# A tuned adaLN block on one core: one tile's exponentials, the second gate's column and its spread moved to other places

## The chip, the core and the metric

The kernel is one program on one core of a Trainium2 chip. Its matrix work is done by TensorE (PE, with PEld for the loading of weights); VectorE (DVE), ScalarE (ACT) and GpSimd (POOL) do the rest, and SyncE (SP) issues most of the DMA transfers. Each engine takes its own instructions in its own order; semaphores tie them together.

The metric is the device time in microseconds of one execution. The kernel before took 769.94 us (median of 3 runs, 769.52 to 769.98).

## The reference

One transformer block on x of 2048 tokens by D = 640, modulated by a condition c. All is in f32.

```python
mod = silu(c) @ w_mod                      # six rows of 640: sa, ca, ga, sb, cb, gb
h = layernorm(x) * (1 + ca) + sa
q, k, v = h @ wqkv                         # 32 heads of 20
phi(z) = concat(softmax(z @ w_phi), softmax(-(z @ w_phi)))    # per head, 40 features
o = (phi(q) @ (phi(k).T @ v)) / (phi(q) @ sum(phi(k)) + 1e-6) # linear attention
x = x + ga * (o @ wo)
h = layernorm(x) * (1 + cb) + sb
out = x + gb * (relu(h @ w1 + b1) ** 2 @ w2 + b2)             # F = 1728
```

Two rows of `mod` matter here: gb, the second gate, by which the MLP's result is multiplied, and b2, the MLP's last bias, which enters as gb * b2.

## The kernel before

Products are made to f32 accuracy from operands that are split into a rounded high part and the remaining low part (`lo` at L87), as three matmuls each. Tokens go in 16 tiles of 128, two tiles to a pair, so there are 8 pairs.

Four stages follow one another. First, up to about 230 us, weights are prepared and every tile gets its k, v and q; phi(k) is accumulated against v, and of phi(q) the exponentials of tiles 0 to 11 are written to DRAM. The last four tiles (`KEPT` = 12 and up, so 12 to 15) keep their q in `EQ`, and their softmax work is done later: `q_chain(t, False)` (DVE: maximum and minimum per head, then two differences, L430 to L433), `exps` (ACT, two exponentials, L436 and L437) and `q_sums` (DVE, sum per head, L478).

Second, a short stretch turns the accumulated products into `kvd`, `kv5` and `zb`. Here the column form of the second gate is begun: `mod_turn(5, ...)` leaves it as `mt5`, one row buffer of the tag s1, of which there are five, and `biases()` reads b2 into another (`b2s`, L510).

Third, the loop over pairs at L1134, in which `b` and `c` are the tiles 2j+5 and 2j+6 that DVE works on ahead of PE. For each tile, `e_prod` (DVE product with zb and a reduction, L877 and L879, then small steps on POOL), `e_recip` and `e_scale` (L892 to L906) make e', the scaled exponentials. For each pair, `tr_e` transposes e' on PE in six groups (`te`, L921), ACT evicts each (`ept`, L923 or L925); `num` multiplies them with kvd and kv5 into the numerator (`numa`, `numb`, `numc`); `num_hi` (ACT, L950) and `num_lo` (DVE, L957) split it into `ot`; and `do_wo` multiplies it with the gated output weights (`pwo`, evicted as `at`, L982). Three PSUM banks are shared by the groups and the numerator. The order of PE, DVE, ACT and POOL in this loop is the order of the program text; SP's order is left to the planner, which goes by its own estimates of when a transfer is ready. `SPREAD` says after which pair a kept tile's `q_chain` and `exps` come, `SUMS` in which pair its `q_sums`. At the end of pair 3, `mod_sum(5, gate_b)` (DVE, L310) sums the turned gate into a column of 5 chunks, and `spread_row` writes this column to DRAM (L328) and reads it back as a row on all partitions, `gb_b` (L329). In pair 5 DVE makes `bb` = b2 * gb_b (L1149). The raw rows of w1 and w2 are loaded by `p_load` (SP, L1004 and L1007), copied by `p_hi` (ACT, L1014) and `p_lo` (DVE). The last pair contains the first layer norm's transposes for the MLP (`t2(0, ...)`, `tb`).

Fourth, from about 389 us to the end, the MLP over pairs j and steps n of two chunks of F each: `up` (PE), its relu and square (ACT L1250, DVE L1251), rounding and low part (`ra`), then the products with w2 one step behind (`acc`, `acc3x`). The order of all five engines is written out by hand for the first pair. `bb` is first used by `add_bias` at step 6 of the first pair, gb_b when the first pair ends.

Of the kernel before, what the change touches and what calls it, by code (L numbers as in the profile page):

```python
# [51 lines left out]
def kernel(  # L52
# [64 lines left out]
    def row(tag, name):  # L117
        return (pc if tag in ("s3", "s4") else mem).tile([P, D], F32, tag=tag, name=name, bufs=BUFS[tag])
# [316 lines left out]
    def exps(e):  # L435
        nc.scalar.activation(e[:, 0], e[:, 0], AF.Exp)  # L436
        nc.scalar.activation(e[:, 1], e[:, 1], AF.Exp, scale=-1.0)  # L437
# [65 lines left out]
            nc.gpsimd.dma_start(w[2 * n : m, 0], w[2 * n : m, 1])  # L503

    ga_b = row("s4", "ga_b")
    b2s = []

    def biases():
        b2s.append(row("s1", "b2s"))
        nc.sync.dma_start(b2s[0], bass.AP(tensor=b2.tensor, offset=b2.offset, ap=[[0, P], [1, D]]))  # L510

    GB = []

# [19 lines left out]
    }  # L533
    gate_a = const.tile([P, NC], F32, name="gate_a")
    gate_b = const.tile([P, NC], F32, name="gate_b")
    LAST_COL = {7: (2, gate_a), 9: (3, cols_b[:, 0:5]), 11: (4, cols_b[:, 5:10])}
    SIDE = {
        2: lambda: mod_mac(2, 0, 1, 2),
# [544 lines left out]
    def t2(j, *ds):  # L1083
        if 0 in ds:
            H2[j] = ht(f"h2_{j}", j, (0, 96))
        if j == 0:
            t_unit(XM[j], cols_b, H2[j], ds[0], f"b{j}", bank(f"tb{j}_{ds[0]}"))
            return
        p = tp(f"tb{j}_{ds[0]}")
        for k, d in enumerate(ds):  # L1090
            t_in(XM[j], d, p[:, 256 * k : 256 * k + 256])
        for k, d in enumerate(ds):
            t_out(cols_b, H2[j], d, f"b{j}", p[:, 256 * k : 256 * k + 256], XX[j][d % 2][:, :256])
# [35 lines left out]
    e_scale(3)  # L1129
    load_e(6)  # L1130
    e_prod(4)
    SPREAD, SUMS = {1: 1, 3: 2}, {2: 1, 4: 2}
    ln0 = None
    for j in range(NB):  # L1134
        nxt = j + 1 < NB
        b, c = 2 * j + 5, 2 * j + 6
        te_at = (0, 1) if 0 < j < 6 else (1, 2)
        if j == 4:
            load_x1(0)
        if j < 5:  # L1140
            p_load()
        if j != 5:
            e_prod(b)
        e_recip(b - 1)
        e_scale(b - 1)
        if j == 5:
            q_chain(KEPT + 3, False)
            add_x(0, 0, 1)
            nc.vector.tensor_tensor(bb, b2s[0], gb_b, op=ALU.mult)  # L1149
            ln0 = ln_parts(XM[0], "b0")  # L1150
        load_e(b + 2)
        def te(at):
            for i, gs in enumerate((range(3), (5, 3, 4))):
                if nxt and te_at[i] == at:
                    tr_e(j + 1, gs)

        do_wo(j, 0, 0)
        te(0)
        if j == 5:
            exps(EQ[KEPT + 3])  # L1160
            q_sums(KEPT + 3)
            e_prod(b)
        do_wo(j, 0, 1)
        if j == 7:
            t2(0, 0)
            t2(0, 1)
        te(1)
        if j == 5 or j == 6:
            next(ln0)
        if j in SUMS:  # L1170
            q_sums(KEPT + SUMS[j])
        e_prod(c)
        if j != 5:
            e_recip(b)
            e_scale(b)
        do_wo(j, 1, 0)
        if j == 7:
            t2(0, 2)
            t2(0, 3)
        te(2)  # L1180
        if nxt:
            num(j + 1)
            num_hi(j + 1)
        do_wo(j, 1, 1, 0, 8)
        if j == 7:
            t2(0, 4)
        if not nxt:
            do_wo(j, 1, 1, 8, 16)
        if nxt:
            do_wo(j, 1, 1, 8, 11)  # L1190
            num_lo(j + 1)
            do_wo(j, 1, 1, 11, 16)
        if j == 5:
            e_recip(b)
            e_scale(b)
        if j in SPREAD:
            q_chain(KEPT + SPREAD[j], False)
            exps(EQ[KEPT + SPREAD[j]])
        if j == 3:
            mod_sum(5, gate_b)  # L1200
            spread_row(1, gate_b, gb_b)
        load_e(c + 2)
        if j == 5:
            next(ln0)
        if 1 <= j < 6:
            p_hi()
        if j == 5:
            p_lo(4)
            p_load(4)
        if j == 6:  # L1210
            p_hi(4)
            p_lo(5)
            p_load(3)
        if j == 7:
            p_load(2)
# [315 lines left out]
    for j in range(NB):  # L1531
        if j <= PLAIN:
            if j:
                by_hand.__exit__(None, None, None)
            by_hand = tc.manual_schedule(engines={ET_.PE, ET_.DVE, ET_.Activation, ET_.Pool} | ({ET_.SP} if j != 1 else set()))
            by_hand.__enter__()
        for n in range(NP):
            down = lambda k: prev and (down_plain if plain(*prev) else down_pair)(*prev, k)
            twice = not plain(j, n)
            m = NP * j + n - NP - 1  # L1540
            if (j, n) == (NB - 1, NP - 1):
                for k in range(2):
                    up(j, 2 * n + k)
                    split_a(j, n, (k,))
                for i in range(2):
                    add(Y[j][i], Y[j][i], XR[j, i])
                break
            done = j - 1 if j and prev else None
            up(j, 2 * n)
            if prev and not plain(*prev):  # L1550
                split_s(*prev)
            down(0)
            if j < PLAIN:
                layer(j + 1, 2 * n, None if j else 0)
            if 0 < m < NP - 2:
                t_split(m - 1)
            if m == -1:
                t_load(0)
            if (j, n) == (PLAIN, 0):
                t_fetch(4)  # L1560
            if j >= PLAIN:
                if n == 5 + (j == PLAIN):
                    for i in range(2):
                        add_bias(j, i)
                layer(j + 1, 2 * n)
            prep(next(PREPS, 0))
            if j == 0:
                layer(j + 1, 2 * n, 1)
            if n == 0 and j:
                if j - 1 >= PLAIN:  # L1570
                    first_combos(j - 1)
                else:
                    Y[j - 1] = [row("s2", f"y{j - 1}_{i}") for i in range(2)]
                for r, i, c in (("3", 0, R), ("2", 0, L)):
                    end(j - 1, r, i, c)
            if n == 1 and j:
                gate(j - 1, 0)
                if j != PLAIN:
                    finish(j - 1, j < PLAIN)
            if n == 1 and j == PLAIN:  # L1580
                finish(j - 1, 0)
            if n == 2 and j == PLAIN:
                t_sums(NP - 2)
            if n == (2 if j > PLAIN else 1) and j:
                gate(j - 1, 1)
            if n == (5, 5, 5, 3)[min(j, 3)]:
                residual(j)
            for i in range(2):
                if n == 6 and j == 0:
                    add_bias(j, i)  # L1590
            if j == NB - 1 and n == 1:
                for k in range(NP - LAST, NP - 1):
                    plain_load(k)
            if j == NB - 1 and n == 3:
                for k in range(NP - LAST, NP - 1):
                    plain_split(k)
            if j == NB - 1 and n == NP - 2:
                for i in range(2):
                    by_gate(Y[j][i], Y[j][i], slice(0, D))
            up(j, 2 * n + 1)  # L1600
            if j >= PLAIN and n == 0:
                down(1)
            split_a(j, n)
            if twice:
                sums(j, n)
            if j < PLAIN or n:
                down(1)
            if m == NP + 1:
                t_split(NP - 2)
            ahead = (j, n) == (0, 3)  # L1610
            if ahead:
                layer(j + 1, 2 * n + 1)
            prep(next(PREPS, 0))
            if n == 0 and j:
                end(j - 1, "4", 1, L)
                end(j - 1, "x", 1, R)
            if n == (2 if j > PLAIN else 1 if j == PLAIN else 0) and j:
                finish(j - 1, j >= PLAIN)
            if not ahead:
                layer(j + 1, 2 * n + 1)  # L1620
            if 0 <= m < NP - 2:
                t_sums(m)
            if m == NP - 2:
                t_split(m - 1)
            if 0 < m + 1 < NP - 1:
                t_load(m + 1)
            if m == NP - 1:
                for i in range(2):
                    add_bias(j - 1, i)
            if j == NB - 1 and n == NP - LAST:  # L1630
                first_combos(j)
            prev = j, n
# [60 lines left out]
```

## Time and profile before

| what | value |
|---|---|
| median of 3 runs | 769.94 us |
| the profiled execution | 769.86 us, span 768.2 us |
| PE busy | 759.3 us (99%) |
| PEld busy | 739.8 us (96%) |
| DVE busy | 593.8 us (77%) |
| ACT busy | 434.6 us (57%) |
| POOL busy | 144.2 us (19%) |
| TensorE clock granted | 1.000 |

Rows of the order of time read: start and duration in us, engine, line of the kernel, operation, tile written and tiles read, shapes, count. A bracket gives the idle time before it and what ended that. Matmuls are pipelined, so a busy PE in such rows overlaps its neighbour, and the distance between two starts is the better measure of what a piece of work takes.

### The profile page before, as it was taken

To read this page: it belongs to the slowest core of one execution; us is meant where nothing else is said; L and a number is where in the kernel's file an instruction comes from. 1 tells how busy PE (TensorE), PEld (TensorE's weight loads), DVE (VectorE), ACT (ScalarE), POOL (GpSimd) and SP (SyncE) were. 2 spreads that over 40 slices of the span, in tenths; PEclk is the share of its full clock that TensorE was granted. 3 is DMA by queue.
4 is the path that set the end of the run, shared out by engine and by line. 5 is a ranking of instruction groups with operands and counts; after the bars stand their busy time and mean duration, and the time that the engine had idled before them with its cause. 6 is when DMAs were issued, how large, how long until landed. Compare 5 with 4: busy or idle time off the path is not lost.

```text
span 768.2 us, 15300 instructions
## 1 busy us (share of the span) xinstructions
PE 759.3 (99%) x5967; PEld 739.8 (96%) x5967; DVE 593.8 (77%) x1083; ACT 434.6 (57%) x971; POOL 144.2 (19%) x301
## 2 busy tenths in 40 slices
PE   9999999999999999999999999999999999999997
PEld 8999999999999989888999999999999999999996
DVE  6598897989999999999565667866767666675666
ACT  5766756767843454545776647465553636445331
POOL 3001101101100255442101000231321313222110
PEclk9999999999999999999999999999999999999999
DMA  9811431343333344155356367996766758766450
GB/s 327 305 65 73 137 103 54 104 139 114 119 104 109 117 142 170 70 80 160 107 180 222 110 226 253 286 323 195 226 181 197 232 177 262 221 184 192 130 165 35
DMA packets 52151, 126.69 MB, mean 165 GB/s; under 512 B 7335, under 2 KB 8103, under 8 KB 52079
## 3 DMA queue, kind: packets, MB, share of 16 engines
q1 hardware_dynamic: 34744, 84.65, 33.1%
q0 software_dynamic: 14752, 35.76, 16.7%
q10 hardware_dynamic: 2583, 5.30, 1.8%
q8 instruction: 47, 0.77, 0.4%
q14 instruction: 25, 0.20, 0.1%
HBM read 95.70 MB, written 29.89 MB: 163 GB/s over the span
## 4 chain that ended last, share of the span: by engine, by line
PE 85%; DVE 8%; issue 2%; DMA 2%; POOL 2%; ACT 1%; SPq 0%; POOLq 0%; DVEq 0%
PE up L78 23%; PE acc L78 17%; PE pk L78 9%; PE pv L78 9%; PE pq L78 8%; PE pwo L78 5%; PE acc3x L78 5%; PE kvp L450 3%; DVE dn L879 2%; DVE scr L877 2%; DVE ezb L901 1%; PE tb L357 1%; PE te L921 1%; DMA ring_b<-td_b 1%; PE ta L357 1%
## 5 line engine op out<-in xcount | busy, mean ns | idle before, releaser
L78 PE MATMUL up<-h,w 128*128 128x256 f32 x1640 | 206.4, 278 | 0.0
L78 PEld LDWEIGHTS up<-h,w 128*128 128x128 f32 x1640 | 196.1, 188 | 0.0
L1250 ACT ACTIVATE ft<-up,b_t 128x256 f32<-128x256 f32 x104 | 48.9, 470 | 115.1 <-PE up L78 114.6
L78 PE MATMUL acc<-w,ra 128*128 128x384 f32 x452 | 97.4, 335 | 0.0
L1251 DVE TENSOR_TENSOR ft<-ft 128x256 f32<-128x256 f32 x104 | 44.1, 424 | 51.2 <-ACT ft L1250 49.6
L78 PE MATMUL pwo<-wo,ot 128*128 128x256 f32 (+3 forms) x512 | 80.8, 312 | 0.6 <-DVE ot L88 0.6
L78 PEld LDWEIGHTS pwo<-wo,ot 128*128 128x128 f32 (+1 forms) x512 | 74.5, 188 | 3.8 <-issue 2.7
L78 PE MATMUL pq<-wq,hT 128*128 128x384 f32 (+1 forms) x480 | 75.2, 312 | 0.0
L78 PEld LDWEIGHTS acc<-w,ra 128*128 128x128 f32 x452 | 72.7, 188 | 0.7 <-DVE ra L88 0.5
L78 PE MATMUL pk<-wk,hT 128*128 128x384 f32 (+1 forms) x480 | 72.7, 308 | 0.0
L78 PE MATMUL pv<-wv,hT 128*128 128x384 f32 (+1 forms) x480 | 71.7, 307 | 0.0
L78 PEld LDWEIGHTS pq<-wq,hT 128*128 128x128 f32 x480 | 71.1, 188 | 0.6 <-issue 0.2
L78 PEld LDWEIGHTS pk<-wk,hT 128*128 128x128 f32 x480 | 70.5, 188 | 0.4 <-issue 0.2
L78 PEld LDWEIGHTS pv<-wv,hT 128*128 128x128 f32 x480 | 70.1, 188 | 0.0
L88 DVE TENSOR_TENSOR ra<-ft,ra 128x384 fp32r<-128x384 f32 (+2 forms) x86 | 36.8, 448 | 32.9 <-ACT ra L1274 20.2
L78 PE MATMUL acc3x<-w,ra 128*128 128x256 f32 x248 | 42.3, 278 | 1.4 <-DVE end L1418 1.4
L1360 POOL DMA_DIRECT2D ring_a<-td_a x34 | 18.3, 537 | 125.5 <-PE acc L78 103.2
L1274 ACT ACTIVATE ra<-ft 128x384 fp32r<-128x384 f32 x48 | 25.2, 526 | 28.4 <-DVE ft L1251 22.4
L78 PEld LDWEIGHTS acc3x<-w,ra 128*128 128x128 f32 x248 | 39.5, 188 | 1.8 <-DVE end L1418 1.6
L1265 DVE TENSOR_TENSOR ft<-ft 128x128 f32<-128x128 f32 x136 | 33.3, 286 | 1.2
L441 DVE TENSOR_REDUCE sk<-ek 128x64 f32<-128x1280 f32 x16 | 23.7, 1484 | 12.4 <-ACT ek L436 10.8
L885 POOL TENSOR_TENSOR dn<-dn,rs_q 128x32 f32<-128x32 f32 x32 | 20.1, 629 | 68.1 <-DVE dn L879 67.8
(264 smaller groups left out, 1406.5 us busy)
## 6 DMA issues: line engine op xcount, KB each, us to landing
ring_c<-td_c POOLq DMA_DIRECT2D x34, 384.0 KB, 4.0
ring_a<-td_a POOLq DMA_DIRECT2D x34, 384.0 KB, 4.1
ring_b<-td_b POOLq DMA_DIRECT2D x34, 256.0 KB, 4.0
esp<-eq SPq DMA_DIRECT2D x12, 640.0 KB, 3.2
el<-esp SPq DMA_DIRECT2D x12, 640.0 KB, 4.0
rw<-in_w SPq DMA_DIRECT2D x23, 320.0 KB, 3.1
wm<-in_w_mod SPq DMA_DIRECT2D x20, 320.0 KB, 3.7
xb<-in_x SPq DMA_DIRECT2D x8, 640.0 KB, 4.0
```

The lines of the kernel that those rows point to most:

```text
L78: nc.tensor.matmul(o, a, b, start=first and i == 0, stop=last and i == len(terms) - 1, skip_group_check=skip,)
L88: (eng or nc.vector).tensor_tensor(out_lo, full, hi.bitcast(F32), op=ALU.subtract)
L357: nc.tensor.transpose(p[:, i * P : (i + 1) * P], xn[:, i, d * P : (d + 1) * P], ident)
L441: nc.vector.tensor_reduce(s, heads(flat(e)), axis=AX.X, op=ALU.add)
L450: nc.tensor.matmul(kvp[g // 4][64 * c : 64 * c + 64, a : a + 2 * n].rearrange("p (s n) -> p s n", s=2), v[:, u], e[:, :, o : o + n], start ...
L877: nc.vector.tensor_tensor(z, flat(ET[t]), flat(zb), op=ALU.mult)
L885: nc.gpsimd.tensor_tensor(dn[:, s], dn[:, s], rs[:, 1 - s], op=ALU.mult)
L1250: nc.scalar.activation(r, p, AF.Relu, bias=b1_t[:, f : f + 1])
L1251: nc.vector.tensor_tensor(r, r, r, op=ALU.mult)
L1265: nc.vector.tensor_tensor(t[:, o], t[:, a], t[:, b], op=op)
L1274: nc.scalar.activation(a[:, 0, :3], t[:, :3], AF.Copy)
L1360: nc.gpsimd.dma_start(RING[j, n, r], TD[n][r].bitcast(F32R))
```

## The change

- `exps` of kept tile 13 move from the end of pair 1 into pair 2, after its second group of e' transposes; the sums of tile 13 (`q_sums`) move from pair 2 to pair 3. Tile 14 keeps its places.
- `mod_sum(5, gate_b)` moves from the end of pair 3 to the start of pair 6.
- Instead of writing the column to DRAM as it stands, TensorE turns it in pair 7 (`gbt`, into the PSUM tile of the tag tp), ACT copies it to a new small tile `gate_r` of 5 rows by 128, and SP writes those rows and reads `gb_b` back.
- b2 is read into `bb` itself, which frees the row buffer of `b2s`; the product bb * gb_b moves from pair 5 to the MLP's first pair, step 4.
- Where the first group of e' transposes comes at place 0 (pairs 1 to 5), the second takes its groups in the order 3, 4, 5 instead of 5, 3, 4.

```diff
     ga_b = row("s4", "ga_b")
-    b2s = []
-
+    
     def biases():
-        b2s.append(row("s1", "b2s"))
-        nc.sync.dma_start(b2s[0], bass.AP(tensor=b2.tensor, offset=b2.offset, ap=[[0, P], [1, D]]))
+        nc.sync.dma_start(bb, bass.AP(tensor=b2.tensor, offset=b2.offset, ap=[[0, P], [1, D]]))
...
     gate_b = const.tile([P, NC], F32, name="gate_b")
+    gate_r = pc.tile([NC, P], F32, name="gate_r")
...
-    SPREAD, SUMS = {1: 1, 3: 2}, {2: 1, 4: 2}
+    SPREAD, SUMS = {1: 1, 3: 2}, {3: 1, 4: 2}
...
         e_recip(b - 1)
         e_scale(b - 1)
+        if j == 6:
+            mod_sum(5, gate_b)
         if j == 5:
             q_chain(KEPT + 3, False)
             add_x(0, 0, 1)
-            nc.vector.tensor_tensor(bb, b2s[0], gb_b, op=ALU.mult)
             ln0 = ln_parts(XM[0], "b0")
         load_e(b + 2)
         def te(at):
-            for i, gs in enumerate((range(3), (5, 3, 4))):
+            for i, gs in enumerate((range(3), (3, 4, 5) if te_at[0] == 0 else (5, 3, 4))):
...
         if j == 5 or j == 6:
             next(ln0)
+        if j == 2:
+            exps(EQ[KEPT + 1])
         if j in SUMS:
             q_sums(KEPT + SUMS[j])
...
         if j == 7:
             t2(0, 4)
+            p = tp("gbt")[:NC, :P]
+            nc.tensor.transpose(p, gate_b, ident)
+            nc.scalar.activation(gate_r, p, AF.Copy)
+            nc.sync.dma_start(GD[1], gate_r)
+            nc.sync.dma_start(gb_b, GD[1].rearrange("c p -> (c p)")[None, :].to_broadcast([P, D]))
...
         if j in SPREAD:
             q_chain(KEPT + SPREAD[j], False)
-            exps(EQ[KEPT + SPREAD[j]])
-        if j == 3:
-            mod_sum(5, gate_b)
-            spread_row(1, gate_b, gb_b)
+            if j > 1:
+                exps(EQ[KEPT + SPREAD[j]])
...
             if not ahead:
                 layer(j + 1, 2 * n + 1)
+            if (j, n) == (0, 4):
+                nc.vector.tensor_tensor(bb, bb, gb_b, op=ALU.mult)
```

## The prediction

> **What bounds the kernel now.** I read the page's first two parts, then busy time by windows over the attention output stage, then the order of time of each engine there, because only an order of time shows which wait ends last. In the page, the second list is the span in 40 slices of 19.2 us; in the windows each row gives PE, PEld, DVE, ACT and POOL busy time.
>
> ```profile
> PE   9999999999999999999999999999999999999997
> DVE  6598897989999999999565667866767666675666
> 300.00:320.00 20.00, 19.59 (x146) 16.79 (x143) 19.62 (x29) 10.45 (x24) 7.64 (x17) 1.00 0.29 100
> 320.00:340.00 20.00, 20.00 (x153) 18.45 (x152) 19.21 (x27) 10.38 (x22) 6.74 (x12) 1.00 0.44 86
> 340.00:360.00 20.00, 19.43 (x141) 17.18 (x142) 19.69 (x32) 9.71 (x21) 6.38 (x11) 1.00 0.58 141
> ```
>
> PE is in its nines everywhere, so the whole program is one long run of matmuls. From about 175 to 365 us DVE is full as well. There the two engines pass work to each other, and a microsecond is won only where PE stands still. So I looked for PE's standstills by comparing the same piece of work in successive pairs (pairs count from 0: pair 2 starts near 304, pair 3 near 319, pair 4 near 334; numerator n belongs to pair n and is made during pair n-1).
>
> ```profile
> 307.36 2.13 PE L78 MATMUL pwo<-wo,ot 128*128 128x256 f32 x16
> 309.82 1.63 PE L921 MATMUL te<-ident,ezb 128*80 128x128 f32 x10 [0.33 <-ACT ept L923]
> 311.20 3.02 PE L78 MATMUL pwo<-wo,ot 128*128 128x384 f32 x16
> ...
> 323.04 2.08 PE L78 MATMUL pwo<-wo,ot 128*128 128x256 f32 x16
> 325.98 3.08 PE L78 MATMUL pwo<-wo,ot 128*128 128x384 f32 x16
> ...
> 331.73 4.89 PE L78 MATMUL pwo<-wo,ot 128*128 128x256 f32 x32
> 336.46 1.48 PE L921 MATMUL te<-ident,ezb 128*120 128x128 f32 x12
> ...
> 346.52 2.46 PE L78 MATMUL pwo<-wo,ot 128*128 128x256 f32 x18
> 349.55 2.71 PE L78 MATMUL pwo<-wo,ot 128*128 128x384 f32 x14 [0.57 <-DVE ot L88]
> 352.11 0.49 PE L921 MATMUL te<-ident,ezb 128*120 128x128 f32 x3
> ```
>
> Output projection half plus second group of e' transposes takes 3.84 us in pair 2 (311.20 - 307.36) and 2.94 in pair 3 (325.98 - 323.04): pair 2 stands still for **0.90 us**, and the bracket names ACT's eviction of e'. Two projection halves up to the next transposes take 5.59 at the end of pair 4 (352.11 - 346.52) and 4.73 at the end of pair 3: **0.86 us** stand still there, for DVE's low part of the numerator. PE can win 1.76 us here, no more.
>
> Now why, from ACT and DVE.
>
> ```profile
> 306.91 0.74 ACT L436 ACTIVATE eq<-eq 128x640 f32<-128x640 f32 x1 [2.99 <-DVE eq L433]
> 308.19 0.72 ACT L1014 ACTIVATE w<-rw 128x640 fp32r<-128x640 f32 x1
> ...
> 315.71 0.60 ACT L950 ACTIVATE ot<-numa 128x512 fp32r<-128x512 f32 x1
> ...
> 311.96 1.47 DVE L478 TENSOR_REDUCE rs_q<-eq 128x64 f32<-128x1280 f32 x1
> ...
> 318.30 0.30 DVE L906 TENSOR_TENSOR ezb<-el,dn 128x80 f32<-128x80 f32 x1
> 318.52 0.68 DVE L88 TENSOR_TENSOR ot<-numa,ot 128x512 fp32r<-128x512 f32 x1
> 320.38 1.47 DVE L877 TENSOR_TENSOR scr<-el,zb 128x1280 f32<-128x1280 f32 x1
> ...
> 330.48 0.29 DVE L906 TENSOR_TENSOR ezb<-el,dn 128x80 f32<-128x80 f32 x1
> 331.19 0.69 DVE L88 TENSOR_TENSOR ot<-numa,ot 128x512 fp32r<-128x512 f32 x1 [0.42 <-ACT ot L950]
> 333.21 0.80 DVE L430 TENSOR_REDUCE mxq<-eq 128x32 f32<-128x640 f32 x1
> 336.37 0.81 DVE L310 TENSOR_REDUCE gate_b<-mt 128x5 f32<-128x640 f32 x1
> 337.10 1.48 DVE L877 TENSOR_TENSOR scr<-eq,zb 128x1280 f32<-128x1280 f32 x1
> ...
> 348.82 0.68 DVE L88 TENSOR_TENSOR ot<-numa,ot 128x512 fp32r<-128x512 f32 x1
> ```
>
> ACT sits 2.99 us in front of the kept tile's exponentials, and e' evictions stand behind them. PE, held up, brings the next numerator late, and DVE then waits 0.42 at 331.19.
>
> **The change, part by part.** The sum is made against the profiled run, 769.86 us (span 768.2), 0.08 under the median 769.94.
>
> *Exponentials of tile 13 from the end of pair 1 into pair 2.* They leave 306.91 and stand behind pair 2's second group of evictions. The copy at 308.19 no longer waits for DVE, evictions start when PE is ready, and the 0.90 us at 309.82 goes. What becomes late next: ACT's eviction of numerator 3, now behind them. The pair costs 1.28 (308.19 - 306.91), so that eviction starts at 315.71 - 0.90 + 1.28 = 316.09 and ends 0.60 later, at 316.69. DVE, without the sum of tile 13 ahead of it, comes at 318.52 - 1.47 = 317.05. Cover 0.36 us, so nothing; uncovered it costs up to the difference, see the rivals.
>
> *Sum of tile 13 from pair 2 to pair 3.* 1.47 us on DVE (311.96) leaves before 318.52 and comes back before 331.19: neutral for numerator 4. Its reader is e_prod(13) in pair 4, still later.
>
> *Effect on DVE at numerator 4.* From L906 to the first instruction after the low parts takes 2.08 in pair 2 (320.38 - 318.30) and 2.73 in pair 3 (333.21 - 330.48). The 0.65 difference is waiting for late PE; PE being 0.90 earlier, it goes: **-0.65 us**.
>
> *Second gate's column sum from pair 3 to pair 6.* DVE loses 337.10 - 336.37 = **-0.73 us** before numerator 5. So DVE reaches 348.82 by 1.38 earlier. PE, 0.90 earlier, still waits there; its wait of 0.86 falls to 0.86 + 0.90 - 1.38 = 0.38. The start at 349.55 moves by 1.38: **DVE, not PE, sets this gain.**
>
> ```profile
> 375.79 0.69 DVE L88 TENSOR_TENSOR ot<-numa,ot 128x512 fp32r<-128x512 f32 x1 [5.75 <-ACT ot L950]
> 423.60 0.42 DVE L1251 TENSOR_TENSOR ft<-ft 128x256 f32<-128x256 f32 x1 [0.34 <-ACT ft L1250]
> 387.83 0.38 PE L357 MATMUL tb<-ident,xm 128*128 128x128 f32 x2
> 387.97 1.19 PE L78 MATMUL pwo<-wo,ot 128*128 128x256 f32 x8
> 389.00 5.28 PE L78 MATMUL up<-h,w 128*128 128x256 f32 x45
> ```
>
> In pair 6 the sum lies in DVE's 5.75 us of idling: nothing; without it, 0.73. The row that it reads keeps its buffer until about 370 instead of 336.37, while b2, read straight into its final place, frees another of the five; one raw weight row then loads later, and its copy stands in the MLP's first pair, after 389.00. Nothing; should it be late after all, ACT waits as in rival C.
>
> *Product of b2 and the gate from pair 5 to the MLP's first pair, n=4.* In pair 5 PE no longer depends on it, so no gain. At its new place it fills the 0.34 idle before 423.60 and pushes that product by about 0.4; the pair's next step, the rounding of both halves, waits for a second product that comes a whole up step later. Nothing; 0.73 if that cover were gone.
>
> *The transposed column.* One TensorE transpose in pair 7, on PE's path. Two transposes hold back the next matmul by 387.97 - 387.83 = 0.14 and their neighbours' gaps bring it near 0.2; the bounds for one are 0.07 and 0.38 (the busy time of two). I take **+0.11**. ACT's small copy and DMA issues are off the path (below).
> The Trainium skill, page "TensorE: Matmul & The Clock Gate", section "Part 4: PE-mode transpose", gives some 275 ns for a transpose inside a kernel; charged in full the total would be 768.8. The row's starts say that neighbours overlap, so I keep the row.
>
> *Order 3, 4, 5 of the e' groups.* The same instructions; the short group goes last and its predecessors find banks free a little later. Between -0.1 and +0.1; taken as 0.
>
> *SP.* The gate's column and its spread leave pair 3 and come at the end of pair 7.
>
> ```profile
> 337.21 0.38 SPq L328 DMA_DIRECT2D gate<-gate_b  x1
> 348.77 0.33 SPq L329 DMA_DIRECT2D gb_b<-gate  x1
> 392.90 0.33 SPq L1004 DMA_DIRECT2D rw<-in_w  x1
> DMA to landing us min/median/max: 3.0/4.5/5.9
> 396.45 1.36 ACT L1014 ACTIVATE w<-rw 128x640 fp32r<-128x640 f32 x2
> 390.92 0.47 ACT L1250 ACTIVATE ft<-up,b_t 128x256 f32<-128x256 f32 x1 [0.78 <-PE up L78]
> ```
>
> The column write as 640 single words held SP's next step for 11.56 us (348.77 - 337.21), with no engine waiting. The new write is five rows. ACT's copy, some 0.4 us by its neighbours, eats into the 0.78 idle before 390.92; with that idle starting at 390.14 the write issues near 390.1 - 1.27 = 388.9. If the spread stands ahead of the raw row now issued at 392.90 (then 391.6), it holds that row once the write takes over 2.7 us. Bounds: 3.0 (the quickest raw row's landing) and 11.56. Five contiguous rows resemble a raw row: 3.0, so the row is 0.3 to 0.7 late. Its copy is the second of 396.45, at about 397.1: 4.2 us after issue, against landings from 3.0. Up to 1.2 of cover: nothing.
> By the Trainium skill, page "DMA: Bandwidth & Descriptors", sections "Specifications" and "Anatomy of one DMA", pieces under 512 B are read, modified and rewritten, and a transfer has a fixed cost of about 2.0 us; the new write has pieces of 512 B. By that SP would not be held at all; the total is the same.
>
> **Sum:** -1.38 + 0.11 = -1.27; 769.86 - 1.27 = 768.6 us, or 0.17% less. Later stages are PE-bound and shift as a whole. The measurement tells about 0.2%, 1.54 us, from no change, and this is under it. Own range 768.2 (the 1.76 us all won, less 0.11) to 769.1 (rival B).
>
> **The rivals.**
> *A: more is won than I count.* For it: PEld is busy 16.79 and 17.18 us in the windows with standstills, 18.45 in the one between; 1.66 + 1.27 = 2.93 us, less 0.11, gives 767.0. Against it: the windows hold different mixes of matmuls, and DVE allows 1.38. Between 767.0 and 768.2.
> The Trainium skill, page "Perfetto Trace Analysis", section "Identifying the Most-Contended Engine", prefers weight-load busy time over matmul busy time as the measure of headroom; that is the reading which gives this rival.
>
> *B: a new wait replaces the old.* If PE does not come the 0.90 earlier in pair 2, numerator 3 is evicted at 315.71 + 1.28 + 0.60 = 317.59, and DVE at 317.05 stands 0.54 us. The gain is 1.38 - 0.54 - 0.11 = 0.73: 769.1. If the 0.65 at numerator 4 also stays, 0.08: 769.8. Against it: ACT's 2.99 idle shows that it was DVE it waited for.
>
> *C: slower, through SP's queue.* If the five-row write takes as long as the column did and the spread stands ahead of the raw row, SP is held to 388.9 + 11.6 = 400.5, the row lands at median 4.5 later, 405, where its copy wanted it at 395.8. ACT stands 9.2 us with all activations of the MLP's next matmuls behind it. PE has at most a stretch like the 45 matmuls of 5.28 us in hand: 3.9 us lost, 772.5. It decides from a write of about 4 us on. For it: a gate write has been that slow. Against: that one was in single words.
>
> *D: placement.* Buffers of small tiles and raw rows move to other addresses and SP's order is the planner's. No row prices this: -0.5 to +2 around the forecast, 769.1 to 770.6 where it costs.
>
> **How the numbers follow.** Forecast 0.58; A 0.12; B 0.15; C 0.06; D 0.09. The likeliest is 768.6. Leaving out C, half of A and half of D gives 767.8 to 769.8. Faster than 768.4: A and a quarter of the forecast, 0.27. Slower than 771.5: C and a little of D, 0.08. The rest, 0.65, is within 0.2%.
>
> **What would show it.** Right: no ACT wait of some 3 us before the first L436 after 303; the second e' group of pair 2 following its projection in about 2.95 us; no DVE wait on numerators 3 and 4; L310 at about 369 inside DVE's idle time; the last pair's up matmuls starting near 387.7 instead of 389.00. Wrong: a DVE wait for ACT's numerator 3; PE's wait at numerator 5 still 0.86 or more; ACT's weight copies waiting for raw rows after 390; a gate write over 4 us.

## The result, and the profile after

| what | before | after |
|---|---|---|
| median of 14 runs each | 769.96 us (769.07 to 771.25) | 768.12 us (767.39 to 769.30) |
| ratio | | 0.998, 95% interval 0.9972 to 0.9987 |
| the profiled execution | 769.86 us, span 768.2 us | 768.32 us, span 766.6 us |

The interval is a gain of 1.0 to 2.2 us; 768.6 was forecast, from a gain of 1.27. In the timelines below, as in the prediction, a row gives start and duration in us, engine, line, operation, tiles, and in a bracket the idle time before it. First the order of time of TensorE in the changed kernel: the pieces of work that the prediction compared, and the one of pair 4.

```profile
307.05 2.08 PE L78 MATMUL pwo<-wo,ot 128*128 128x256 f32 x16
...
309.98 3.08 PE L78 MATMUL pwo<-wo,ot 128*128 128x384 f32 x16
...
336.34 2.08 PE L78 MATMUL pwo<-wo,ot 128*128 128x256 f32 x16
338.57 1.39 PE L920 MATMUL te<-ident,ezb 128*120 128x128 f32 x10 [0.15 <-ACT ept L922]
339.72 3.07 PE L78 MATMUL pwo<-wo,ot 128*128 128x384 f32 x16
...
345.46 5.29 PE L78 MATMUL pwo<-wo,ot 128*128 128x256 f32 x32
350.58 1.47 PE L920 MATMUL te<-ident,ezb 128*120 128x128 f32 x12
```

Pair 2's half and second group now take 2.93 us (309.98 - 307.05) where they took 3.84: the standstill there is gone. In pair 4 the same piece takes 3.38 (339.72 - 336.34), and the bracket names ACT's eviction of e'. At the end of pair 4, two halves up to the next transposes take 5.12 (350.58 - 345.46) instead of 5.59; 0.39 over the unhindered 4.73 is still lost. The kernel before, TensorE in pair 4:

```profile
337.69 2.13 PE L78 MATMUL pwo<-wo,ot 128*128 128x256 f32 x16
...
340.78 3.07 PE L78 MATMUL pwo<-wo,ot 128*128 128x384 f32 x16
```

So pair 4 took 3.09 before (340.78 - 337.69), and 0.29 us of standstill is new there. Now the order of time of ACT, then of DVE, in the changed kernel.

```profile
313.69 0.38 ACT L924 ACTIVATE ept<-te 80x256 f32<-80x256 f32 x1 [2.65 <-PE numa L78]
313.97 0.72 ACT L436 ACTIVATE eq<-eq 128x640 f32<-128x640 f32 x1
...
315.60 0.59 ACT L949 ACTIVATE ot<-numa 128x512 fp32r<-128x512 f32 x1
...
335.66 0.74 ACT L436 ACTIVATE eq<-eq 128x640 f32<-128x640 f32 x1 [2.75 <-DVE eq L433]
```

```profile
316.95 0.68 DVE L88 TENSOR_TENSOR ot<-numa,ot 128x512 fp32r<-128x512 f32 x1
...
330.52 0.68 DVE L88 TENSOR_TENSOR ot<-numa,ot 128x512 fp32r<-128x512 f32 x1
...
347.27 0.68 DVE L88 TENSOR_TENSOR ot<-numa,ot 128x512 fp32r<-128x512 f32 x1
...
368.12 0.82 DVE L310 TENSOR_REDUCE gate_b<-mt 128x5 f32<-128x640 f32 x1
374.21 0.69 DVE L88 TENSOR_TENSOR ot<-numa,ot 128x512 fp32r<-128x512 f32 x1 [5.28 <-ACT ot L949]
...
421.69 0.82 DVE L1627 TENSOR_TENSOR bb<-bb,gb_b 128x640 f32<-128x640 f32 x1
422.43 0.42 DVE L1256 TENSOR_TENSOR ft<-ft 128x256 f32<-128x256 f32 x1
423.93 0.43 DVE L88 TENSOR_TENSOR h<-xx,h 128x256 fp32r<-128x256 f32 x1 [1.09 <-ACT h L369]
```

Tile 13's exponentials follow the sixth e' group with no idle time (313.97), and numerator 3 is still evicted by 316.19 (315.60 + 0.59), 0.76 us ahead of DVE's 316.95. No bracket stands at numerators 3 and 4. DVE reaches numerator 5 at 347.27 instead of 348.82. The column sum lies in idle time, which shrank from 5.75 to 5.28, and the product of b2 pushes one product, ahead of 1.09 us of idling. The last fences: SP and TensorE around the gate's write.

```profile
388.46 0.28 SPq L1192 DMA_DIRECT2D gate<-gate_r  x1
389.65 0.33 SPq L1193 DMA_DIRECT2D gb_b<-gate  x1
391.42 0.33 SPq L1003 DMA_DIRECT2D rw<-in_w  x1
```

```profile
386.47 0.27 PE L1190 MATMUL gbt<-ident,gate_b 128*5 128x128 f32 x1
386.50 1.18 PE L78 MATMUL pwo<-wo,ot 128*128 128x256 f32 x8
387.51 5.28 PE L78 MATMUL up<-h,w 128*128 128x256 f32 x45
```

The five-row write let SP's next step go after 1.19 us (389.65 - 388.46), and the raw row stands at 391.42, 1.48 earlier than before's 392.90, as everything around it is.

**How the two traces are compared below.** The same matmul has a start in each trace. From the difference I take off the difference at matmul 100 (counted from 0; 14.82 us before): the first weights land at slightly different times, which moved the whole program by -0.54 to +0.45 us in the profiles of this study and says nothing of a change. "Net" means that. There is one profile of each kernel; from 60 to 290 us, ahead of every moved piece, the nets of all of them lie within 0.04 us of zero. At matmul 2760 (350.53 before, just behind pair 5's start) the changed kernel is **1.31 us** ahead net; ahead of pair 2's second group 0.10, behind it 0.94, in pair 3's last projection 1.12, at the end of pair 4 0.84, in the MLP after the turn 1.25, at the end 1.32. In between, from about 490 us on, the difference shifts by half a microsecond and comes back near 515 us, at a wait for a ring transfer (`ring_b`, weights of the MLP that GpSimd reads back from DRAM), so I judge by the net at pair 5 and use medians for the total.

### The profile page after: what moved, and what is told of

The parts are those of the page before. It is cut to its first block, busy times and chain, and to the rows that moved or that the text cites. A ratio compares the mean times of both kernels' runs of the same rounds, so it can differ in the third digit from the quotient of the medians.

```text
span 766.6 us, 15303 instructions
## 1 busy us (share of the span) xinstructions
PE 759.5 (99%) x5968; PEld 740.5 (97%) x5968; DVE 593.9 (77%) x1083; ACT 435.6 (57%) x972; POOL 144.9 (19%) x301
## 4 chain that ended last, share of the span: by engine, by line
PE 85%; DVE 8%; DMA 2%; issue 2%; ACT 1%; POOL 0%; SPq 0%; POOLq 0%; DVEq 0%; ACTq 0%
PE up L78 21%; PE acc L78 16%; PE pq L78 9%; PE pk L78 9%; PE pv L78 9%; PE pwo L78 6%; PE acc3x L78 4%; PE kvp L450 3%; PE te L920 1%; DVE dn L878 1%; DVE scr L876 1%; DVE ezb L900 1%; PE tb L357 1%; PE foldk L280 1%; DMA ring_b<-td_b 1%
```

## The experiments

**e1: tile 13 alone.** The kernel before with its exponentials and sums moved; the gate and the order of the groups as they were.

```diff
-    SPREAD, SUMS = {1: 1, 3: 2}, {2: 1, 4: 2}
+    SPREAD, SUMS = {1: 1, 3: 2}, {3: 1, 4: 2}
...
+        if j == 2:
+            exps(EQ[KEPT + 1])
...
-            exps(EQ[KEPT + SPREAD[j]])
+            if j > 1:
+                exps(EQ[KEPT + SPREAD[j]])
```

> The kernel before with one part of the change: tile 13's exponentials in pair 2 and its sums in pair 3; gate, b2 and the order of the groups as before. Theory (DVE sets the gain): PE no longer stands still in pair 2 (3.84 us from projection half to projection half falls to about 2.95, so PE is 0.90 earlier), but the start of pair 5's projection (349.55 before) moves only by DVE's 0.65, and PE's wait there grows from 0.86 to about 1.1. Whole: about -0.65 us. Rival A (PE's standstills are all that counts): the start of pair 5 moves by 0.90. Rival B (new wait for numerator 3): DVE waits for ACT at numerator 3 and less than 0.4 is won.

Measured: 768.60 us (before, same chip: 769.65), ratio 0.9985 (0.9976 to 0.9994). Net it is -0.83 behind pair 2's second group and -1.01 in pair 3, but at pair 5 only **-0.63**. TensorE's order of time in e1 says why:

```profile
337.18 2.13 PE L78 MATMUL pwo<-wo,ot 128*128 128x256 f32 x16
...
340.62 3.07 PE L78 MATMUL pwo<-wo,ot 128*128 128x384 f32 x16
...
349.38 0.78 PE L78 MATMUL pwo<-wo,ot 128*128 128x384 f32 x3 [0.57 <-DVE ot L88]
```

TensorE comes earlier and stands again: 3.44 us in pair 4 (340.62 - 337.18) and 0.57 for DVE's numerator 5. What is won is what DVE wins (0.65 by the forecast), not the 0.90 that TensorE no longer stood. One thing came otherwise than I expected: the wait at pair 5 did not grow to 1.1 us (its bracket is 0.57 in both kernels). The rest of the 0.90 is lost in pair 4 already, 3.44 us against 3.09 before, where ACT's evictions stand behind tile 14's exponentials, and those wait for DVE.

**e2: the gate alone.** The changed kernel with tile 13's work and the order of the groups put back.

```diff
-    SPREAD, SUMS = {1: 1, 3: 2}, {3: 1, 4: 2}
+    SPREAD, SUMS = {1: 1, 3: 2}, {2: 1, 4: 2}
...
-        if j == 2:
-            exps(EQ[KEPT + 1])
...
-            if j > 1:
-                exps(EQ[KEPT + SPREAD[j]])
+            exps(EQ[KEPT + SPREAD[j]])
```

> The kernel before with the other part alone: the gate's sum in pair 6, its column turned, b2 read into place, product in the MLP; exponentials, sums and the order of the groups as before. Theory: PE's standstill of 0.90 in pair 2 stays, DVE's wait of 0.42 at numerator 4 stays, the start of pair 5 moves by 0.73, and with 0.11 for the turn about -0.6 us in the whole. Together with the other part alone this adds up to the 1.38 of the whole change, since both are DVE time before the same handover. Rival (PE is the limit): the parts don't add up to the whole.

Measured: 769.22 us, ratio 0.9993 (0.9983 to 1.0002); the interval holds 1, so the times alone do not show this gain. The net does: **-0.64** at pair 5. (In the one profile of e2 it is given back near 515 us, at a wait of 1.3 us for `ring_b`; the net at the end is +0.14.) In e2's order of time of TensorE pair 2 stands as before: 3.91 us.

```profile
306.88 2.13 PE L78 MATMUL pwo<-wo,ot 128*128 128x256 f32 x16
...
310.79 1.49 PE L78 MATMUL pwo<-wo,ot 128*128 128x384 f32 x7
...
346.14 5.03 PE L78 MATMUL pwo<-wo,ot 128*128 128x256 f32 x32
351.01 1.26 PE L920 MATMUL te<-ident,ezb 128*120 128x128 f32 x10
```

The two parts add up: -0.63 - 0.64 = -1.27 against -1.31 for the whole. In e2 the wait at pair 5's start fell by 0.72, nearly the 0.73 of the sum: 4.87 us lie between 346.14 and 351.01, 0.14 over the unhindered 4.73, where it was 0.86.

**e6 and e7: which engine sets pair 5's start?** To the changed kernel, e6 adds a second, useless column sum on DVE at the end of pair 3; e7 does one matmul of 384 columns twice in pair 4 (its first result is overwritten). A single run each.

```diff
+        if j == 3:
+            mod_sum(5, gate_b)
```

```diff
+        if (j, i, h) == (4, 1, 0):
+            mm(PWO[t][h][:, :n], terms[:1])
         mm(PWO[t][h][:, :n], terms[a:b], first=(a == 0), last=(b == 16))
```

> The changed kernel with the column sum done twice: once more at its old place, the end of pair 3. Theory: 0.73 us more on DVE ahead of numerator 5 comes out whole, the start of pair 5's projection is 0.7 later against the run's own start than in the changed kernel, and PE's wait there grows from 0.25 to about 1 us. Rival A (DVE has room): less than 0.3.

> The changed kernel with one matmul of 384 columns (0.17 us) done twice in pair 4, ahead of numerator 5. Theory: it fits into PE's wait of 0.25 us at the start of pair 5's projection, which moves by under 0.05. Rival A (PE is the limit): it moves by 0.17.

Measured: e6 is at -0.64 net instead of -1.31, **0.67** lost for the 0.73 that DVE got; 769.18 us. In e7 the same matmuls lie 0.10 to 0.15 us later than in the changed kernel behind the doubled one, and 0.03 earlier at pair 5: the wait there swallowed it whole; 768.06 us. At this place and of this size, DVE's time costs and TensorE's does not. The row of e6 at pair 5:

```profile
348.90 2.71 PE L78 MATMUL pwo<-wo,ot 128*128 128x384 f32 x14 [0.81 <-DVE ot L88]
```

**e5: the sum left in pair 2.** The changed kernel with `q_sums` of tile 13 where it was, right behind the exponentials' new place.

```diff
-    SPREAD, SUMS = {1: 1, 3: 2}, {3: 1, 4: 2}
+    SPREAD, SUMS = {1: 1, 3: 2}, {2: 1, 4: 2}
```

> The changed kernel with tile 13's sums left in pair 2, the exponentials in pair 2 as changed. Theory: the sums reach DVE at about 311.8 but the exponentials end at 315.3, since ACT does them behind an eviction that waits for a bank or a row; DVE stands 3.5 us, numerators 3 to 5 come later by as much less what was idle, the start of pair 5 moves by +3.2 against the changed kernel, and the whole is 2.5 to 3.5 us slower than the changed kernel. Rival (DVE is not the limit here): under 1 us slower.

Measured: 773.67 us, ratio 1.0048 (1.0031 to 1.0065): 5.5 us over the changed kernel, 2 more than the upper end of what I expected. One row of DVE, two of TensorE, and busy time by windows (PE, PEld, DVE, ACT, POOL, then the granted clock):

```profile
315.52 1.49 DVE L478 TENSOR_REDUCE rs_q<-eq 128x64 f32<-128x1280 f32 x1 [3.54 <-ACT eq L437]
```

```profile
315.90 2.46 PE L78 MATMUL pwo<-wo,ot 128*128 128x256 f32 x18
322.82 4.26 PE L78 MATMUL pwo<-wo,ot 128*128 128x384 f32 x14 [4.46 <-DVE ot L88]
```

```profile
318.00:322.00 4.00, 0.36 (x3) 0.04 (x1) 3.90 (x7) 1.12 (x2) 1.91 (x3) 1.00 0.21 82
322.00:326.00 4.00, 3.18 (x12) 3.18 (x13) 3.96 (x7) 0.00 (x0) 0.81 (x4) 0.69 0.00 0
326.00:330.00 4.00, 4.00 (x32) 3.90 (x30) 3.93 (x7) 2.01 (x4) 2.82 (x4) 0.88 0.00 0
```

DVE's wait is as expected (3.54), and TensorE stands 4.46 for it. At pair 5 the net is +4.45, 5.8 us behind the changed kernel where I expected 3.2. What I had not counted is the clock: the 14 matmuls behind the standstill take 4.26 us, where the 14 at the same place of pair 5 before took 2.71. That is about 1.5 of the 2.6 us; the rest is the standstill, which I had reckoned too short. So the exponentials' move is only good together with the sum's.

**e3: the old order of the e' groups** (5, 3, 4) in the changed kernel, a single run.

```diff
-            for i, gs in enumerate((range(3), (3, 4, 5) if te_at[0] == 0 else (5, 3, 4))):
+            for i, gs in enumerate((range(3), (5, 3, 4))):
```

> The changed kernel with the groups of e' in the old order 5, 3, 4. Theory: in pair 4, where the second group already stands 0.25 to 0.3 us for evictions, the old order stands 0.1 to 0.3 us more, since its short group has two transposes ahead of the next bank instead of four; the start of pair 5's projection does not move (within 0.1 us), because DVE's low part sets it. Rival: the order is worth its 0.2 us in the whole, and the start of pair 5 moves by it.

Measured: 768.72 us; net -1.34 at pair 5 against -1.31. In pair 4 it is some 0.2 behind the changed kernel, as expected, but there DVE decides. The order is worth nothing in the time here. It does change the cover at numerator 3: ACT evicts that numerator at 316.30 in e3 and ends 0.60 later, DVE comes at 317.29, so 0.39 us are left, where the changed kernel has 0.76.

**e4: no turn.** The changed kernel, but the column is written as it stands, as 640 single words.

```diff
-            p = tp("gbt")[:NC, :P]
-            nc.tensor.transpose(p, gate_b, ident)
-            nc.scalar.activation(gate_r, p, AF.Copy)
-            nc.sync.dma_start(GD[1], gate_r)
-            nc.sync.dma_start(gb_b, GD[1].rearrange("c p -> (c p)")[None, :].to_broadcast([P, D]))
+            spread_row(1, gate_b, gb_b)
```

> The changed kernel, with the gate's column written to DRAM as it stands (640 words) instead of being turned, in the same pair 7. Theory: the planner can issue the write as soon as the sum is there (about 369 us), in a stretch where SP waits anyway; the write takes about 11.5 us, no raw row is late, the total stays within 0.3 us of the changed kernel's and the turn's 0.11 on PE is saved. Rival C (SP held): the write comes at the end of pair 7, the raw rows of the MLP's first steps wait behind it, ACT waits for one, and the time is 3 to 8 us longer.

Measured: 767.85 us, ratio 0.9976 (0.9966 to 0.9985), net -1.32 at pair 5 and -1.37 behind pair 7, where the changed kernel, after its turn, is at -1.25. It is no slower than the changed kernel. SP in e4:

```profile
369.95 0.50 SPq L328 DMA_DIRECT2D gate<-gate_b  x1
379.58 0.33 SPq L329 DMA_DIRECT2D gb_b<-gate  x1
381.71 0.33 SPq L1003 DMA_DIRECT2D rw<-in_w  x1
```

The write again put off the read-back of the row, for 9.6 us. But with no turn in pair 7 to wait for, the planner put it right behind the sum of pair 6, in a stretch in which no raw row is due. So e4 does not tell what a slow write costs where it is in the way. e9 does.

**e9: the slow write in the way.** As e4, with the column sum, too, taken only in pair 7. A single run.

```diff
-        if j == 6:
-            mod_sum(5, gate_b)
...
-            p = tp("gbt")[:NC, :P]
-            nc.tensor.transpose(p, gate_b, ident)
-            nc.scalar.activation(gate_r, p, AF.Copy)
-            nc.sync.dma_start(GD[1], gate_r)
-            nc.sync.dma_start(gb_b, GD[1].rearrange("c p -> (c p)")[None, :].to_broadcast([P, D]))
+            mod_sum(5, gate_b)
+            spread_row(1, gate_b, gb_b)
```

> The changed kernel, with the column sum taken in the last pair, right where the changed kernel turns the column, and written as 640 single words from there, instead of the turn. In the column-form run above the write lay in an idle stretch of SP (369.95), so it could not show what SP's queue costs; here it must issue near 388. Rival C as forecast: SP is held some 10 us with a raw weight row behind it, ACT's copy of that row stands, the matmuls of the MLP's first pair lose 3 to 4 us, total about 771 to 772. My own reading: the rows behind it have cover, since the copies that want them stand in an order with other work; if a row that is 9 us late still costs under 1 us, total about 768.5 to 769.0. If the spread is issued behind the raw rows, nothing moves, 768.0 to 768.3.

Measured: **778.91 us**; net -1.36 ahead of the MLP, +9.50 at 425 us. Rival C's 3 to 4 us fall short by far, and my own reading, that the rows have cover, fell. SP, ACT, TensorE and the windows of e9 (behind the granted clock stand the busy share of the DMA engines and the GB/s that they moved):

```profile
389.80 0.38 SPq L328 DMA_DIRECT2D gate<-gate_b  x1
390.23 0.67 SPq L1006 DMA_DIRECT2D rw<-in_w  x1
402.11 0.33 SPq L329 DMA_DIRECT2D gb_b<-gate  x1
402.52 1.26 SPq L1003 DMA_DIRECT2D rw<-in_w  x1
```

```profile
403.12 0.74 ACT L1013 ACTIVATE w<-rw 128x640 fp32r<-128x640 f32 x1 [7.85 <-DMA rw<-in_w]
406.67 0.74 ACT L1013 ACTIVATE w<-rw 128x640 fp32r<-128x640 f32 x1 [2.81 <-DMA rw<-in_w]
```

```profile
398.38 1.86 PE L78 MATMUL up<-h,w 128*128 128x256 f32 x15
409.20 1.33 PE L78 MATMUL acc<-w,ra 128*128 128x384 f32 x3 [8.96 <-ACT ra L1274]
```

```profile
394.00:400.00 6.00, 6.00 (x51) 6.00 (x49) 2.32 (x4) 1.27 (x3) 0.00 (x0) 1.00 0.51 27
400.00:406.00 6.00, 0.24 (x3) 0.04 (x1) 0.82 (x1) 0.74 (x1) 0.00 (x0) 0.71 0.50 135
406.00:412.00 6.00, 2.79 (x10) 2.71 (x11) 3.91 (x8) 4.10 (x8) 0.00 (x0) 0.50 1.00 361
```

The spread goes out 12.31 us behind the write (402.11 - 389.80); SP issues one raw row at once behind the write (390.23) and then nothing until the spread. ACT stands 10.66 for two raw rows, TensorE 8.96, and then runs at half its clock for about 3 us. The second of the late rows was issued after the spread. The first had been issued at 390.23, ahead of it, and was still missing until 403, though SP was not holding it. The trace's records of single packets show that it waited in the transfers themselves: the single words of the write are recorded from 390.75 to 391.23, and the row's 128 packets begin at 391.53, but single ones take up to 9.7 us and the last ends at 402.80. In the window of 394 to 400 us the DMA engines are busy for 0.51 of the time and move 27 GB/s; in the changed kernel it is 0.75 and 237 GB/s. So the transfer behind the slow write was late as well, not only SP's next issues. Why the packets took so long is not shown.

**e8: take away the waits that are left.** The changed kernel with tile 14's exponentials between the two e' groups of pair 4, and its sum and denominator behind numerator 5 (`e_den` holds the small steps with which `e_prod` ended). In pair 5, tile 15's `q_chain` and `add_x` move along, ahead of `e_recip`.

```diff
-    SPREAD, SUMS = {1: 1, 3: 2}, {3: 1, 4: 2}
+    SPREAD, SUMS = {1: 1, 3: 2}, {3: 1}
...
+        if j == 5:
+            q_sums(KEPT + 2)
+            e_den(KEPT + 2)
+            q_chain(KEPT + 3, False)
+            add_x(0, 0, 1)
         e_recip(b - 1)
...
+        if j == 4:
+            exps(EQ[KEPT + 2])
         do_wo(j, 0, 1)
...
-            if j > 1:
-                exps(EQ[KEPT + SPREAD[j]])
```

> The changed kernel and one step more: tile 14's exponentials between the two groups of pair 4's transposes instead of before them, and its sums, with the small steps on POOL that need them, behind numerator 5. Theory: that takes 1.4 us of DVE time from ahead of numerator 5 and the evictions' delay from PE; both standstills that are left (0.25 to 0.3 us in pair 4, 0.25 at pair 5) go, the start of pair 5 is some 0.5 us earlier than in the changed kernel, and then PE has no wait left there: the whole gains 0.5, not 1.4. About 767.6 us. Rival (DVE alone): 1.4 us. Rival (a new wait): DVE waits for tile 14's exponentials or POOL, nothing is won.

Measured: 767.49 us (767.10 to 767.74), ratio 0.9968 (0.9956 to 0.998), net **-2.08** at pair 5. TensorE's order of time in e8 has neither wait: 2.93 us in pair 4 (339.56 - 336.63) and 4.72 at its end (350.04 - 345.32).

```profile
336.63 2.08 PE L78 MATMUL pwo<-wo,ot 128*128 128x256 f32 x16
...
339.56 3.08 PE L78 MATMUL pwo<-wo,ot 128*128 128x384 f32 x16
...
345.32 4.89 PE L78 MATMUL pwo<-wo,ot 128*128 128x256 f32 x32
350.04 1.48 PE L925 MATMUL te<-ident,ezb 128*120 128x128 f32 x12
```

The sum of 1.47 us that left DVE's way bought 0.77: no more than TensorE's own standstills, which are all gone now. That is more than the 0.5 that I expected, because those standstills were larger than I had taken them: 0.44 in pair 4 (3.38 - 2.94) and 0.39 at pair 5. This kernel has the lowest median of all; its interval overlaps with those of the changed kernel and of e4.

**e10: e8 with the column form of e4.**

> The fastest kernel so far (exponentials of tile 14 between the two e' groups of pair 4, its sum and denominator after numerator 5) with the column form of the gate, its write in SP's idle stretch near 370, instead of the turn. If the turn costs 0.1 us of TensorE time and the column form nothing, pair 7 onward is 0.1 earlier and the total is 767.3 to 767.5, ratio to the kernel before 0.996 to 0.9975; by the other theory, that the column write delays raw rows, 768 or more.

Measured: 767.73 us (766.35 to 769.03), ratio 0.9967 (0.9955 to 0.9979). Not to be told from e8, and its profile, net -2.11 at pair 5, gave back 0.9 past 500 us, most of it near a wait for `ring_b`. Behind pair 7 its net is -2.13 against -2.00 in e8, so the turn's 0.1 us is saved there, but the times of these runs cannot show it.

## Why the prediction was right, point by point

- **What bounds, and pair 2.** Right: 2.93 us instead of 3.84, where about 2.95 was to be seen.
- **Numerator 3, rival B.** The feared wait did not come. The eviction began at 315.60, not 316.09, and the cover was 0.76, not 0.36. Of the 0.49, 0.23 is the earlier start of the whole trace. The rest comes from the order of the groups: the one that ACT evicts ahead of the exponentials is now the short one, 0.28 from 313.69 to 313.97, where a long one took 0.49 before. That I had not seen. e3, with the old order, has a cover of 0.39, so my 0.36 was right for that order.
- **Numerator 4.** Right: the 0.42 bracket of 331.19 is gone at 330.52.
- **The column sum, and "DVE, not PE, sets this gain".** Right. At pair 5 1.31 was won where the sum said 1.38; e1 and e2 give 0.63 and 0.64 for its terms 0.65 and 0.73. e6 and e7, a single run each, show the claim directly. The rest of TensorE's wait, forecast as 0.38, is 0.39.
- **What the sum did not see.** Pair 4's new 0.29 us. Tile 14's exponentials now stand in front of ACT there (ACT idles 2.75 us for DVE ahead of 335.66), exactly as tile 13's did in pair 2, because TensorE comes sooner; e1 has this wait too. It cost nothing, since DVE was later still at pair 5; e8, which takes away both, won 0.77 more. It also breaks the cap of 1.76 "and no more": e8 won 2.08. I had counted the two large standstills and left out small ones: 0.15 in pair 4 (3.09 against 2.94) and 0.1 to 0.2 around pair 2's ends.
- **The turn.** +0.11 forecast, +0.11 in the net (-1.36 to -1.25). The row shows 0.27 us of busy time; the Trainium skill, page "TensorE: Matmul & The Clock Gate", section "Part 4: PE-mode transpose", gives some 275 ns for a block of 128 by 128 in bf16 inside a kernel, and agrees as a duration (the ends of matmuls are modelled in the profile), but the next matmuls start 0.03 behind it.
- **SP's write, the mis-sized term.** Taken as 3.0 us, with 3.0 as the lower bound; it took **1.19**. The bound came from the landing of a raw row of 320 KB, while the gate has 2.5 KB, and a larger transfer is no lower bound for a smaller one. So the raw row was not late at all, instead of 0.3 to 0.7; the total is unmoved. Whether there was cover for a row 0.3 to 0.7 late was not tried. The fixed cost of 2.0 us that the prediction sets beside it is the figure that the Trainium skill, page "DMA: Bandwidth & Descriptors", section "Anatomy of one DMA", fits for transfers issued by GpSimd; this one, issued by SP, took less. One reading of the lines was wrong too: the 11.56 us before were not "SP's next step". SP had issued a raw row at 337.69, between write and spread, and its packets, as in e9, lasted until 349.86. No engine wanted it then, so nothing stood.
- **b2's product and the order of the groups.** Right: both cost nothing in the time.
- **Rival A.** The time lies in the range that I gave it, but its reading fell: the weight loads' busy time in 340 to 360 us is 17.21 now against 17.18, though 0.47 us of standstill left that window. The changed kernel's row:

```profile
340.00:360.00 20.00, 19.91 (x148) 17.21 (x148) 19.73 (x28) 11.04 (x23) 6.62 (x10) 1.00 0.31 116
```

- **Rival C.** The mechanism is real and was averted by the five-row write; e9 adds what it left out, that a row issued ahead of the spread is late as well. Its price was 3.9 and is 10.9 (-1.36 to +9.50). ACT was to stand 9.2 us and stood 10.7. The failed term is what TensorE has in hand: 5.28 forecast, but it stood for 8.96 of these 10.7, so under 2 us. The slower clock behind it, some 1.7 more, was not in the sum. That it decides from a write of about 4 us on was not tried.
- **Rival D.** Nothing of it up to 287 us, where the two traces lie within 0.02 net. Past 490 us it is not ruled out, see the total.
- **The total.** The median fell by 1.84, the net in the profile by 1.32 at its end. The interval of 1.0 to 2.2 holds both. So the net gain, 1.25 behind the turn, is the forecast 1.27, while the median 768.12 lies just under my own range of 768.2 to 769.1, in the range of rival A, by half a microsecond that no part of my sum explains. TensorE's wait for `ring_b` near 515 us is 0.7 us in the profile before, 0.2 in the changed kernel's, 1.3 in e2's and nothing in e8's; I could not show that such waits account for the rest, and it stays open.

## What to carry to other kernels

Where two full engines hand work to each other, a wait removed on one is worth only what the other arrives earlier: compute both arrivals at the next handover and take the later one, then look for the next instruction that now stands early in a queue in front of what is needed. A reduction that stands right behind its activation has to move with it: e5 lost 5.5 us by leaving it. A slow transfer is priced by what is queued behind it, on the issuing engine and in the transfers, and not by its length: the same write was free in an idle stretch and cost 10.9 us where weight rows were due.

## What the hardware showed that I had not expected

A standstill of TensorE costs more than its length. After 4.46 us (e5) the granted clock was 0.69 and 0.88 in the next two windows; after 8.96 us (e9) it was 0.50 over a whole window. Cut finer, the windows read 0.50 from 323.60 to 326.80 in e5 and from 402.60 to 412.60 in e9, and 1.00 on both sides, so those means are windows with both. The waits of up to 1.3 us in the other runs left it at 1.00. The Trainium skill, page "TensorE: Matmul & The Clock Gate", section "Part 1: The HAM clock gate (the "warmup" mystery)", says that the clock falls to half after an idle window of about 3.4 us. The two levels agree. The length does not come out of these rows: in e9 the clock is 1.00 up to 402.40 and 0.50 from 402.60, some 2.3 us after the last matmul ended (398.38 + 1.86 = 400.24), and in e5 it falls only after the matmuls have begun again, between 323.40 and 323.60.

The gate's 2.5 KB put off the read-back behind them by 1.19 us as five rows and by 9.6, 11.56 and 12.31 us as 640 words. The Trainium skill, page "DMA: Bandwidth & Descriptors", section "Rules for kernel authors", says that a non-contiguous last dimension becomes one descriptor per element and should be rearranged; the ratio of eight to ten, by these rows, agrees in direction, and the page gives no figure for it.
